# One attention and two expert layers on one core: the order of the whole program taken from a list scheduler written into the kernel, with buffers placed by hand

## The chip, the cores and the metric

One Trainium2 chip, one core of it. The metric is the device time in microseconds of one execution on that core. The kernel before takes 1005.12 us (median of 3 runs, 1003.41 to 1005.69).

## The reference

```python
# attention, batch 4, heads 8, sequence 576, head size 64
q_d, k_d, v_d = means over 4 neighbouring positions (144 of them)
out_up    = repeat(softmax(q_d k_d^T / 8) v_d, 4)
out_local = softmax(where(|i-j| < 4, q k^T / 8, -1e9)) v
x = (out_up + out_local)                     # 2304 tokens x 512
# first expert layer, 512 -> 1536 -> 512
xn = x / sqrt(mean(x*x) + 1e-6) * rms_g
g = xn @ w_gate
x = (g * sigmoid(g) * (xn @ w_val)) @ w_out
# second expert layer, 512 -> 2048 -> 512
r = maximum(x @ w_in, 0)
out = (s * (r * r) + b) @ w_out2
```

The first softmax is over scores with their row maximum subtracted, and its sum has 1e-9 added. The second layer's weights are called in_moe_w_in (or moe2_w_in) and in_moe_w_out among the kernel's inputs, like those of the first.

## The kernel before

The 2304 tokens are 8 blocks of 288. Activations lie transposed (features on partitions). Float32 products are made of fp16 halves: each operand is split into a high half (ACT, L133) and a low half (DVE, L134; or POOL, L136), and three fp16 products are accumulated. Weights arrive as 8-byte numbers: each 128-row piece is staged by a DMA (L476) and narrowed by two ACT and two DVE instructions (L480, L481, L485, L487); a product of the weights' upper halves with themselves ("gram", L515 for the first layer, L870 for the second) gives a bound from which the scale of the split is taken, so that no split can start before its part's gram.

- **Attention** runs per batch `b` and pair of heads (a "unit", 4 per batch): scores of the local windows (L357 and L361, tile sl), their maximum and its subtraction on DVE (L263, L264), exponent on ACT, sums and division; downsampled scores (L387, sd); transposes (L371, L407); products with the values (L278 for the downsampled ones, pvd, 12 matmuls on values that POOL has summed over 4 rows; L292 for the local ones, pl); then per half batch a norm (L425 to L451), whose factor is spread over the partitions by nine bf16 matmuls (L441). During batch 0 dummy matmuls (L319, `warm`) are issued in fixed numbers.
- **First expert layer, "moe1"** (L577 and L600): per block 24 groups of 12 matmuls 128x288 for gate and value (12 pairs), tanh on ACT and two products on DVE (L585, L187; tile u), halves of the result by ACT (L588) and POOL (L589), then 4 groups of 36 matmuls for the output. Blocks 0 and 1 run together part by part (4 weight parts), then blocks 2 to 5 singly, then 6 and 7 together. At a block's end a sum of squares (tile sn, L620) gives the scale of its result.
- **Second expert layer, "stage 2"** (L1123): a seven-product Strassen scheme on 2x2 blocks, so that a block of tokens takes 56 products of 12 matmuls 128x144; the first 28 (tiles bmm, bc) make the hidden values of four parts p, and the last 28 (by, bc) the outputs. Between them DVE and ACT form sums (L1141, L1145), squares, and halves (L1152, L1150). The eight weight parts, q0 to q3 of w_in and q4 to q7 of w_out2, each give 14 pieces 128x256, which are split after the part's gram. The halves of the hidden values need a scale (gsc, L895) that takes the grams of all eight parts.

**What sets the order.** The first 50 steps of the loop of blocks 0 and 1 (`run_first`, `ORDERED`) and all before them are ordered by the framework's own scheduler. After that PE's order is the program's, where generators of the main chain, of attention and of weight preparation are interleaved by hand-set numbers (`LAG_*`, `UNIT_STEP`, `START2`, ...; L35 to L60). Stage 2 is ordered by a small list scheduler `Plan` (PE, ACT and DVE; L1030 to L1085) with prices written into each call.

## Time and profile before

| what | value |
|---|---|
| median of the runs | 1005.12 us (1003.41 to 1005.69, n=3) |
| profiled execution, its own time | 1004.8 us |
| its span on the core | 1002.9 us |
| mean granted TensorE clock | 0.968 of full speed |
| busy: PE / DVE / ACT / POOL | 939.8 / 706.1 / 611.0 / 249.2 us |
| first moe1 matmul, first stage-2 matmul | 91.5, 653.5 us after the span's start |

The span runs from the first to the last instruction; the profiled execution's own time is 1.9 us longer. Busy time is the time in which an engine executes anything; overlapping instructions are counted once. The granted clock is TensorE's, as a share of 2.4 GHz.

### The profile page before, as it was taken

To read this page: it belongs to the slowest core of one execution; us is meant where nothing else is said; L and a number is where in the kernel's file an instruction comes from. 1 tells how busy PE (TensorE), PEld (TensorE's weight loads), DVE (VectorE), ACT (ScalarE), POOL (GpSimd) and SP (SyncE) were. 2 spreads that over 40 slices of the span, in tenths; PEclk is the share of its full clock that TensorE was granted. 3 is DMA by queue.
4 is the path that set the end of the run, shared out by engine and by line. 5 is a ranking of instruction groups with operands and counts; after the bars stand their busy time and mean duration, and the time that the engine had idled before them with its cause. 6 is when DMAs were issued, how large, how long until landed. Compare 5 with 4: busy or idle time off the path is not lost.

```text
span 1002.9 us, 27332 instructions
## 1 busy us (share of the span) xinstructions
PE 939.8 (94%) x11467; PEld 809.9 (81%) x11467; DVE 706.1 (70%) x1643; ACT 611.0 (61%) x1517; POOL 249.2 (25%) x341
## 2 busy tenths in 40 slices
PE   5975888979999999999999999689999999999998
PEld 3654766758877887878877888489999999999998
DVE  4997997764345244278686778879678796787966
ACT  2766687543444334356555555686769687686875
POOL 8524675544446333420211221000000000000000
PEclk9975999989999999999999999799999999999999
DMA  8982336211111100023220322000000000000000
GB/s 245 286 244 57 106 109 187 63 50 57 55 49 38 50 15 2 1 85 95 75 85 2 102 68 86 22 2 9 20 26 2 25 8 20 26 2 25 8 20 26
DMA packets 25580, 61.45 MB, mean 61 GB/s; under 512 B 3216, under 2 KB 11408, under 8 KB 25456
## 3 DMA queue, kind: packets, MB, share of 16 engines
q1 hardware_dynamic: 25456, 59.70, 19.6%
q8 instruction: 90, 1.47, 0.6%
q14 instruction: 34, 0.28, 0.1%
HBM read 54.97 MB, written 4.72 MB: 60 GB/s over the span
## 4 chain that ended last, share of the span: by engine, by line
PE 69%; DVE 16%; ACT 6%; DMA 3%; issue 3%; POOL 2%; SPq 0%; ACTq 0%; DVEq 0%; POOLq 0%
PE bc L1123 14%; PE mmb L577 13%; PE bmm L1123 12%; PE mmb L600 8%; PE by L1123 7%; DVE W L134 4%; PE m2b L577 4%; ACT W L133 2%; DVE u L585 1%; DVE u L187 1%; PE pl L292 1%; PE tpl L371 1%; PE m2b L600 1%; PE sl L361 1%; DVE W L487 1%
## 5 line engine op out<-in xcount | busy, mean ns | idle before, releaser
L1123 PEld LDWEIGHTS <-W 128*128 128x128 f16 x4704 | 297.2, 98 | 3.6 <-issue 3.6
L577 PEld LDWEIGHTS <-W 128*128 128x128 f16 x2304 | 223.3, 98 | 62.1 <-issue 5.4
L577 PE MATMUL mmb<-X,W 128*128 128x288 f16 x1752 | 236.3, 288 | 3.7 <-DVE u L585 1.9
L600 PEld LDWEIGHTS <-W 128*128 128x128 f16 x1152 | 113.1, 100 | 44.2 <-issue 8.0
L1123 PE MATMUL bmm<-W,W 128*128 128x144 f16 x1920 | 131.8, 226 | 1.6 <-DVE R L1141 1.6
L589 POOL TENSOR_TENSOR R<-u,R 128x288 f16<-128x288 f32 x96 | 78.1, 814 | 202.0 <-ACT R L588 186.1
L600 PE MATMUL mmb<-R,W 128*128 128x288 f16 x864 | 114.9, 289 | 6.6 <-DVE z L266 5.8
L588 ACT ACTIVATE R<-u 128x288 f16<-128x288 f32 x96 | 42.3, 441 | 87.1 <-DVE u L187 86.9
L1123 PE MATMUL bc<-W 128*128 128x144 f16 x1152 | 77.2, 226 | 0.0
L577 PE MATMUL m2b<-X,W 128*128 128x288 f16 x552 | 75.1, 286 | 0.0
L1152 DVE SCALAR_TENSOR_TENSOR W<-R,gsc,W 128x288 f16<-128x288 f32 x136 | 68.1, 511 | 4.5 <-ACT W L1150 4.5
L1150 ACT ACTIVATE W<-R,gsc 128x288 f16<-128x288 f32 x136 | 68.8, 523 | 3.1 <-DVE R L1141 2.1
L134 DVE SCALAR_TENSOR_TENSOR W<-W,wis 128x256 f16<-128x256 f32 x98 | 46.5, 505 | 23.2 <-ACT W L133 23.2
L1145 ACT ACTIVATE R<-R 128x288 f32<-128x288 f32 x160 | 62.7, 431 | 0.1
L585 DVE SCALAR_TENSOR_TENSOR u<-u,mmb 128x288 f32<-128x288 f32 x50 | 22.5, 450 | 55.7 <-PE mmb L577 52.8
L1123 PE MATMUL bc<-W,W 128*128 128x144 f16 x768 | 58.5, 226 | 1.7 <-ACT x L606 1.7
L1123 PE MATMUL by<-W 128*128 128x144 f16 x864 | 59.2, 228 | 0.0
L133 ACT ACTIVATE W<-W,wis 128x256 f16<-128x256 f32 x98 | 45.6, 500 | 19.0 <-DVE W L134 10.5
L1141 DVE TENSOR_TENSOR R<-bmm,R 128x288 f32<-128x288 f32 x72 | 32.6, 454 | 33.8 <-PE bmm L1123 21.9
L584 ACT ACTIVATE u<-mmb,tsc 128x288 f32<-128x288 f32 x96 | 47.1, 490 | 13.5 <-PE mmb L577 13.2
L487 DVE SCALAR_TENSOR_TENSOR W<-W,R 128x512 int32<-128x512 int32 (+1 forms) x53 | 46.4, 876 | 2.4 <-ACT W L480 1.3
L485 DVE SCALAR_TENSOR_TENSOR R<-R 128x512 int32<-128x512 int32 (+1 forms) x57 | 41.7, 733 | 7.7 <-ACT R L481 7.5
(260 smaller groups left out, 1606.8 us busy)
## 6 DMA issues: line engine op xcount, KB each, us to landing
R<-in_moe_w_out_dram SPq DMA_DIRECT2D x26, 512.0 KB
R<-in_moe_w_in_dram SPq DMA_DIRECT2D x16, 512.0 KB
qkT<-in_qk_dram SPq DMA_DIRECT2D x14, 576.0 KB
vw<-in_vwin_dram SPq DMA_DIRECT2D x14, 315.0 KB
vd<-in_vgrp_dram SPq DMA_DIRECT2D x13, 288.0 KB
W<-in_moe_w_gate_dram SPq DMA_DIRECT2D x9, 384.0 KB
R<-in_moe_w_val_dram SPq DMA_DIRECT2D x8, 384.0 KB
W<-in_moe_w_val_dram SPq DMA_DIRECT2D x8, 384.0 KB
```

Source lines behind the costliest of these rows:

```text
L133: act.activation(out=hi, in_=src, func=AF.Copy, scale=scale)
L134: dve.scalar_tensor_tensor(out=lo, in0=src, scalar=scale, in1=hi, op0=ALU.mult, op1=ALU.subtract)
L487: dve.scalar_tensor_tensor(out=di, in0=di, scalar=3, in1=stg[:, :, 0], op0=ALU.logical_shift_left, op1=ALU.bitwise_or)
L577: pe.matmul(out=acc, lhsT=Cgv.half(o, FP, lw)[:, f0 * 128:f0 * 128 + 128], rhs=X16[:, kc, 3 * blk:3 * blk + 3, lx, :], start=i == 0, stop= ...
L584: act.activation(out=u, in_=ps[0], func=AF.Tanh, scale=tsc[:, part:part + 1])
L588: act.activation(out=hi, in_=u, func=AF.Copy)
L589: pool.tensor_tensor(out=lo, in0=u, in1=hi, op=ALU.subtract)
L600: pe.matmul(out=acc, lhsT=Co.half(fc * 512, 512, lw)[:, m * 128:(m + 1) * 128], rhs=g16(fc)[:, lx, :], start=i == 0, stop=i == 35)
L1123: pe.matmul(out=p[:, m, :], lhsT=t[:, a:a + 128], rhs=x[:, i, lx, k, :], start=first and m == k == lw == lx == 0, stop=last_ and k == 1 an ...
L1145: plan.add(ACTe, lambda: act.activation(out=slot(o), in_=get(a), func=func), [nm(a)], [o], 0.34 if psum else 0.42, 0.45 if psum else 0.52)
L1150: plan.add(ACTe, lambda: act.activation(out=dst[:, i, 0], in_=s(), func=AF.Copy, scale=scale), [sn], [f"{dn}{i}h"], 0.43, 0.6)
L1152: plan.add(DVEe, lambda: dve.scalar_tensor_tensor(out=dst[:, i, 1], in0=s(), scalar=scale, in1=dst[:, i, 0], op0=ALU.mult, op1=ALU.subtrac ...
```

## The change

Every operation of the kernel (five engines: PE, ACT, DVE, POOL and SP's DMA issues) is no longer issued but recorded, with the spans of memory that it reads and writes (a PSUM bank counts as one). `schedule` gives each a duration by a formula, runs a list scheduler backward for due times and forward for the order, twice, and `emit` issues everything in that order, engine by engine. The main chain of matmuls (moe1 and stage 2) keeps the program's own order; everything else may go around it. Operations marked `either` go to DVE or POOL as the scheduler finds. DVE operations with two SBUF inputs and POOL operations are never scheduled at the same time. Dependences are those of the recorded order of the program: an operation that writes a buffer comes after all earlier ones that read it there.

All buffers are fixed: PSUM banks are MM (4), SB_ (2) and XV (2), handed out in turn by `take`; for blocks 5 to 7 moe1 also uses SB_ and the first XV bank. The grams and the sums sn use XV. `AREA` holds the attention's buffers first and the w_in parts later.

Three pieces of arithmetic move. For batches 0 and 1 (`PE_SUM`) the subtraction of the maximum is a float32 matmul with a negative identity (128x350 and 128x280), and the sum of 4 value rows is taken by 48 instead of 12 pvd matmuls per unit. The norm's factor is spread by three float32 matmuls instead of nine bf16 ones. The dummy matmuls become fillers that `emit` puts into gaps of the planned PE order before the first chain matmul.

DVE has 1755 instructions instead of 1643, POOL 143 instead of 337; PE's, ACT's and SP's numbers change little. All recorded operations are issued from line L292, fillers from L1033.

```diff
-ORDERED = 50
...
+PE_SUM = (0, 1)
...
+    def record(self, engs, name, args, kw):
+        if self.AP is None:
+            self.AP = type(args[0] if args else kw["out"])
...
+        for e in engs:
+            if e == "DVE":
+                occ = 0.065 + 1.042e-3 * n + (0.06 if scal else 0)
+                alts.append((e, occ, occ + 0.15, len(big) > 1 and n > 32))
+            elif e == "ACT":
+                psum = any(a.space == PSUM for a in ins)
+                occ = 0.06 + (0.85e-3 if psum else 0.95e-3) * n + 0.1 * scal + (0.09 if "accum_out" in kw else 0)
+                alts.append((e, occ, occ + 0.17, False))
+            elif e == "POOL":
+                occ = (0.9 if kw.get("op") == ALU.pow else 0.2) if n < 32 else 0.08 + 2.1e-3 * n * (0.9 if n > 500 else 1)
+                alts.append((e, occ, occ + 0.15, n >= 32))
...
+    def pe_time(self, name, kw):
+        n = cols(kw["out"])
+        rhs = kw.get("rhs", kw.get("in_"))
+        k = rhs.ap[0][1]
+        if name == "transpose":
+            return 0.11
+        if rhs.dtype == F32:
+            return 4 * n / 2.4e3 + 0.004 if k > 72 and n > 8 else 0.112 if k > 72 else n / 2.4e3 + 0.01
+        return n / 2.4e3 + 0.0024
...
+        while len(order) < n:
+            best = None
+            for e in engs:
+                w = wait[e]
+                w[:] = [x for x in w if not done[x[1]]]
+                ok = [x for x in w if e != "PE" or not self.ops[x[1]].chain or x[1] == chain[at]]
+                if not ok:
+                    continue
+                t = max(free[e], min(x[0] for x in ok))
+                lok = [x for x in ok if x[0] <= t + 1e-9]
+                k, i = min(((x[1], x[2]) for x in lok), key=lambda x: (key[x[0]], x[0]))
+                a = self.ops[k].alts[i]
+                ts = max(t, port) if a[3] else t
+                if a[3] and port > t + 0.05:
+                    other = [(x[1], x[2]) for x in lok if not self.ops[x[1]].alts[x[2]][3]]
+                    if other:
+                        k, i = min(other, key=lambda x: (key[x[0]], x[0]))
+                        ts = t
+                if best is None or ts < best[0] - 1e-9:
+                    best = (ts, e, k, i)
+            t, e, k, i = best
+            a = self.ops[k].alts[i]
+            done[k] = True
+            free[e] = t + a[1]
+            if a[3]:
+                port = t + a[1]
+            start[k], where[k] = t, i
+            if self.ops[k].chain:
+                at += 1
+            order.append(k)
+            for j in succ[k]:
+                if back:
...
+        for _ in range(rounds):
+            s, _w, _o, _t = self.run(succ, pred, chain[::-1], key, True)
+            late = [-(s[k] + self.ops[k].alts[0][1]) for k in range(n)]
+            start, where, order, t = self.run(pred, succ, chain, late, False)
+            if best is None or t < best[3]:
+                best = (start, where, order, t)
+            key = [-x for x in start]
...
+        for k in order:
+            o = self.ops[k]
+            e = o.alts[where[k]][0]
+            if e == "PE":
+                gap = start[k] - free
+                if free > until and start[k] <= first and gap > 0.5:
+                    for _ in range(int(0.7 * gap / 0.22)):
+                        filler()
+                free = start[k] + o.alts[0][1]
+            for name, args, kw in o.fn:
+                getattr(self.real[e], name)(*args, **kw)
...
+    MM, SB_, XV = bank[0:4], bank[4:6], bank[6:8]
...
-    def sum4(vd, vs=None):
-        pool.tensor_tensor(out=vd[:, :, 0:2, :], in0=vd[:, :, 0:2, :], in1=vd[:, :, 2:4, :], op=ALU.add)
-        if vs is None:
-            vs = ap.tile([72, 4, D], F32, tag="vs", name="vs", bufs=2)
-        pool.tensor_tensor(out=vs, in0=vd[:, :, 0, :], in1=vd[:, :, 1, :], op=ALU.add)
-        return vs
...
-        dve.tensor_tensor(out=a, in0=src, in1=zb, op=ALU.subtract)
...
+        if b in PE_SUM:
+            pe.matmul(out=src, lhsT=neg_f, rhs=zb, start=False, stop=True, skip_group_check=True)
+            act.activation(out=a, in_=src, func=AF.Exp, scale=1.0 / 8)
+        else:
+            dve.tensor_tensor(out=a, in0=src, in1=zb, op=SUB)
...
-    def warm(b, t, n):
-        if b < WARMB:
-            for _ in range(n):
-                pe.matmul(out=t, lhsT=ones_b, rhs=warm_in[:, :t.shape[1]], start=True, stop=True, skip_group_check=True)
...
+        if b not in PE_SUM:
+            pool.tensor_tensor(out=v4[:, :, 0:2, :], in0=v4[:, :, 0:2, :], in1=v4[:, :, 2:4, :], op=ADD)
+            vs = take("vs", VS)[:72].rearrange("p (a d) -> p a d", a=4)
+            pool.tensor_tensor(out=vs, in0=v4[:, :, 0, :], in1=v4[:, :, 1, :], op=ADD)
+            parts = [[vs[:, a, :]] for a in range(4)]
+        else:
+            parts = [[v4[:, a, r, :] for r in range(4)] for a in range(4)]
+        pvd = (take("mm0", MM[:3]) if b == 0 else take("xv", XV))[:, :SD]
...
+                        pe.matmul(out=pvd[64 * h:64 * h + 64, c0:c0 + n], lhsT=v,
...
-                pe.matmul(out=rb[:, c * GR:(c + 1) * GR], lhsT=rp[i][:, c:c + 1].to_broadcast([GR, 128]),
-                          rhs=ident_b[:GR, :GR], start=i == 0, stop=i == 2)
...
+                pe.matmul(out=rb[:, c * GR:(c + 1) * GR], lhsT=r[:, c:c + 1].to_broadcast([GR, 128]),
+                          rhs=ident_f[:GR, :GR], start=True, stop=True)
...
+    def mm_bank(t):
+        if wide_mm[0]:
+            return take("mmw", MM + SB_ + [XV[0]])
+        return take("mm", MM)
...
+            act.activation(out=g[:, fc, 0, :], in_=u, func=AF.Copy)
+            either.tensor_tensor(out=g[:, fc, 1, :], in0=u, in1=g[:, fc, 0, :], op=SUB)
...
+    HOME = [(AREA, q * PART) for q in range(4)] + [(W1, q * PART) for q in range(3)] + [(R, 0)]
...
-        first = mains((0, 1))
-        sides.append(attn(1))
-        run_first(first, 0, ORDERED)
-        order[0] = tc.manual_schedule(engines={pe.engine})
-        order[0].__enter__()
-        run_first(first, ORDERED, 1000)
...
+    for hp in range(NP):
+        unit(0, hp)
+    for hh in range(2):
+        norm(0, hh)
+    def attention(b):
+        for hp in range(NP):
+            unit(b, hp)
+        for hh in range(2):
+            norm(b, hh)
+    prep_gv(0)
+    g = [g16_of(0), g16_of(1)]
+    for part in range(NPART):
+        if part:
+            prep_gv(part)
+        for blk in range(2):
+            moe1_gv(blk, g[blk], part)
+    prep_out()
+    attention(1)
+    for blk in range(2):
+        moe1_out(blk, g[blk])
+    for blk in range(2, NB - 2):
+        if blk in (2, 3):
+            attention(blk)
+        if blk == NB - 3:
+            wide_mm[0] = True
+            for q in range(4):
+                prep_part(q)
+        g = g16_of(blk)
+        for part in range(NPART):
+            moe1_gv(blk, g, part)
+        moe1_out(blk, g)
+    g = [g16_of(0), g16_of(1)]
+    for part in range(NPART):
+        for i in range(2):
+            moe1_gv(NB - 2 + i, g[i], part)
+    for i in range(2):
+        moe1_out(NB - 2 + i, g[i])
+    x_ops(0)
+    for q in range(4, 8):
+        prep_part(q)
+    part_scales()
     for blk in range(NB):
         in_stage(blk)
         if blk == 0:
-            last_post()
-            finish_out2()
+            bias()
         if blk < NB - 1:
             x_ops(blk + 1)
         y_stage(blk)
-    plan.emit()
-    order[0].__exit__(None, None, None)
-    tail["pw"].__exit__(None, None, None)
...
+    with tc.manual_schedule(engines={nc.tensor.engine, nc.scalar.engine, nc.vector.engine, nc.gpsimd.engine, nc.sync.engine}):
+        plan.emit(filler, 4.0)
```


In the order of instructions, three places. The first is DVE around the first use of moe1's gate and value results, before and after. Names: W is the weights' space, R and u are working buffers (R also holds staging), rs the scales of the gate and value splits, gvh, gvs, gvi the steps of a scale, tsc the factor of the tanh. A 128x384 operation with rs is a low half of a gate or value piece; one without is a narrowing.

Before, from the first low half on (the first u operation, L585, is row 161, with the narrowings of part 1 and the norm of the second half batch between):

```order
134 L134 SCALAR_TENSOR_TENSOR W_82<-W_82,rs 128x384
135 L183 TENSOR_SCALAR gvi<-gvs 128x2
136 L521 TENSOR_SCALAR rs<-rms_sb,gvs 128x4 x2
137 L296 TENSOR_TENSOR X<-pl,od 128x256
138 L134 SCALAR_TENSOR_TENSOR W_82<-W_82,rs 128x384
139 L522 TENSOR_SCALAR tsc<-gvi 128x1
140 L187 SCALAR_TENSOR_TENSOR invg<-gvi 128x1
141 L134 SCALAR_TENSOR_TENSOR W_82<-W_82,rs 128x384 x6
142 L296 TENSOR_TENSOR X<-pl,od 128x320
143 L134 SCALAR_TENSOR_TENSOR W_82<-W_82,rs 128x384 x7
144 L296 TENSOR_TENSOR X<-pl,od 128x256
145 L134 SCALAR_TENSOR_TENSOR W_82<-W_82,rs 128x384
```

After, the start of the splits, and the piece up to the first u operations (rows 183 and 187):

```order
139 L292 TENSOR_SCALAR rs<-rms_sb,gvs_162 128x4
140 L292 TENSOR_REDUCE m_152<-bank_101 128x1
141 L292 SCALAR_TENSOR_TENSOR W_85<-W_85,R 128x384
142 L292 TENSOR_SCALAR rs<-rms_sb,gvs_162 128x4
143 L292 TENSOR_SCALAR gvi_163<-gvs_162 128x2
144 L292 TENSOR_REDUCE m_152<-bank_100 128x1
145 L292 SCALAR_TENSOR_TENSOR W_85<-W_85,rs 128x384 x4
146 L292 TENSOR_SCALAR m_152<-m_152,rmax 128x2
147 L292 SCALAR_TENSOR_TENSOR W_85<-W_85,rs 128x384
```

```order
176 L292 SCALAR_TENSOR_TENSOR W_85<-W_85,rs 128x384 x7
177 L292 TENSOR_REDUCE AREA<-bank_100 128x3
178 L292 TENSOR_SCALAR rs<-rms_sb,gvs_165 128x4
179 L292 SCALAR_TENSOR_TENSOR W_85<-W_85,rs 128x384
180 L292 TENSOR_SCALAR AREA<-AREA 128x3
181 L292 SCALAR_TENSOR_TENSOR W_85<-W_85,rs 128x384 x2
182 L292 SCALAR_TENSOR_TENSOR R<-R 128x512
183 L292 SCALAR_TENSOR_TENSOR u_89<-u_89,bank_95 128x288
184 L292 SCALAR_TENSOR_TENSOR W_85<-W_85,R 128x512
185 L292 SCALAR_TENSOR_TENSOR W_85<-W_85,rs 128x384
186 L292 TENSOR_SCALAR AREA<-AREA 128x3
187 L292 SCALAR_TENSOR_TENSOR u_89<-u_89,bank_94 128x288
```

The narrowings of all four parts (64 operations 128x384 on DVE) and 26 of the 32 low halves now stand ahead of the first complete u; before, 59 narrowings and 16 low halves on DVE did.

The second place is DVE at the start of stage 2. Before (L134 are the last 14 of the 112 low halves 128x256, L1141 is stage 2's first sum, gsc the scale of the hidden values):

```order
861 L187 SCALAR_TENSOR_TENSOR mm__8409<-invj,ivw 128x4
862 L892 TENSOR_REDUCE big<-mm__8409 128x1
863 L893 TENSOR_SCALAR big<-big 128x1
864 L895 TENSOR_SCALAR gsc<-mm__8409,big 128x4
865 L134 SCALAR_TENSOR_TENSOR R<-R,wis 128x256 x14
866 L187 SCALAR_TENSOR_TENSOR c_8469<-s_sb,big 128x1
867 L187 SCALAR_TENSOR_TENSOR cy<-cx,c_8469 128x7
868 L1141 TENSOR_TENSOR R<-bmm,R 128x288 x3
869 L1141 TENSOR_TENSOR R<-bc,R 128x288
870 L1141 TENSOR_TENSOR R<-bmm,R 128x288
871 L1141 TENSOR_TENSOR R<-bc,R 128x288 x2
872 L1152 SCALAR_TENSOR_TENSOR W_82<-R,gsc,W_82 128x288
```

After, the start of stage 2 (mo is the maximum of block 7's sn, mi that of a gram in bank 100 or 101, the row with bank_95 is stage 2's first sum) and then the place of gsc:

```order
945 L292 TENSOR_REDUCE mo<-bank_101 128x1
946 L292 TENSOR_SCALAR poh_180<-mo 128x1
947 L292 TENSOR_SCALAR pos_181<-poh_180 128x1
948 L292 TENSOR_REDUCE mi<-bank_100 128x1
949 L292 TENSOR_TENSOR W_85<-W_85 128x2x256
950 L292 TENSOR_SCALAR wih_183<-mi 128x1
951 L292 TENSOR_TENSOR W_85<-W_85 128x2x256
952 L292 TENSOR_SCALAR wis_184<-wih_183 128x1
953 L292 TENSOR_REDUCE mi<-bank_101 128x1
954 L292 TENSOR_TENSOR R<-bank_95,R 128x288
955 L292 SCALAR_TENSOR_TENSOR W_85<-W_85,wis_184 128x256 x2
956 L292 TENSOR_SCALAR wii_185<-wis_184 128x1
```

```order
1008 L292 TENSOR_REDUCE big<-mm_157 128x1
1009 L292 SCALAR_TENSOR_TENSOR R<-R,wis_187 128x256
1010 L292 TENSOR_SCALAR big<-big 128x1
1011 L292 SCALAR_TENSOR_TENSOR W_85<-W_85,wis_184 128x256
1012 L292 TENSOR_SCALAR gsc<-mm_157,big 128x4
1013 L292 SCALAR_TENSOR_TENSOR W_85<-W_85,wis_184 128x256
1014 L292 SCALAR_TENSOR_TENSOR R<-R,wis_187 128x256 x2
1015 L292 SCALAR_TENSOR_TENSOR W_85<-R,gsc,W_85 128x288 x5
1016 L292 SCALAR_TENSOR_TENSOR W_85<-W_85,wis_184 128x256 x2
1017 L292 SCALAR_TENSOR_TENSOR R<-R,wis_187 128x256
```

Before, 98 of the 112 low halves stand ahead of gsc and of stage 2's first sum; now 56 stand ahead of the first sum, and the other 56 (rows 955 to 1062) between it and the first output product, with gsc at row 1012 among them. Between row 954 and row 1070, where the last halves stand that the first output product takes, there are these 56 low halves, 29 low halves of stage-2 operands, 38 sums 128x288, and 24 others, 147 in all.

## Rows read from the trace of the kernel before

**Rows 1.** The page: busy time of each engine.

```profile
PE 939.8 (94%) x11467; PEld 809.9 (81%) x11467; DVE 706.1 (70%) x1643; ACT 611.0 (61%) x1517; POOL 249.2 (25%) x341
```

**Rows 2.** Windows, five stages: stretch, length, busy (instructions) by engine, PEclk, DMA share, GB/s.

```profile
0.00:91.50 91.50, 62.15 (x709) 43.44 (x710) 71.80 (x162) 51.60 (x131) 47.70 (x70) 0.80 0.73 219
91.50:217.20 125.70, 109.45 (x1161) 84.44 (x1160) 105.86 (x227) 87.67 (x219) 73.79 (x82) 0.96 0.36 109
217.20:600.00 382.80, 380.69 (x3727) 305.40 (x3728) 214.84 (x490) 183.47 (x449) 124.30 (x186) 0.99 0.17 51
600.00:664.00 64.00, 52.85 (x475) 42.29 (x473) 51.10 (x120) 39.73 (x94) 3.38 (x4) 0.92 0.14 42
664.00:998.60 334.60, 334.60 (x5401) 334.34 (x5398) 262.06 (x645) 247.59 (x628) 0.00 (x0) 0.99 0.05 15
```

**Rows 3.** Timeline, PE, moe1's first matmuls and the wait of block 0's output: start, us, what.

```profile
91.53 1.84 PE L577 MATMUL mmb<-X,W 128*128 128x288 f16 x7 [1.09 <-ACT X L450]
...
210.24 1.14 PE L577 MATMUL mmb<-X,W 128*128 128x288 f16 x8
217.20 0.66 PE L600 MATMUL mmb<-R,W 128*128 128x288 f16 x2 [5.82 <-DVE z L266]
```

**Rows 4.** Windows, the start, columns as in rows 2.

```profile
0.00:75.00 75.00, 56.06 (x654) 39.19 (x655) 59.61 (x139) 43.23 (x113) 40.18 (x58) 0.86 0.86 258
75.00:91.50 16.50, 6.08 (x55) 4.25 (x55) 12.18 (x25) 8.37 (x19) 7.52 (x12) 0.50 0.12 41
```

**Rows 5.** Timeline, DVE: neighbours in a dense stretch.

```profile
60.10 0.55 DVE L485 SCALAR_TENSOR_TENSOR R<-R 128x384 int32<-128x384 int32 x1
60.57 0.43 DVE L263 TENSOR_REDUCE z<-sl 128x4 f32<-128x280 f32 x1
...
61.01 0.52 DVE L485 SCALAR_TENSOR_TENSOR W<-W 128x384 int32<-128x384 int32 x1
61.45 0.54 DVE L487 SCALAR_TENSOR_TENSOR W<-W,R 128x384 int32<-128x384 int32 x1
```

**Rows 6.** Windows, line L577 alone: PE and PEld busy (instructions).

```profile
91.50:217.20 125.70, 79.11 (x576) 55.78 (x575) 0.96 0.36 109
```

**Rows 7.** Chain that ended last, two of its pieces: start, us, what.

```profile
457.19 4.41 PE mmb L600 x36
461.60 4.42 PE m2b L600 x36
```

**Rows 8.** Timeline, PE: value sums and downsampled scores of one unit.

```profile
326.58 0.88 PE L278 MATMUL pvd<-PdT,vs 72*64 72x64 f32 x24
327.39 1.89 PE L600 MATMUL mmb<-R,W 128*128 128x288 f16 x14
...
312.29 0.95 PE L387 MATMUL sd<-qd 64*64 64x144 f32 x12
313.17 1.03 PE L577 MATMUL mmb<-X,W 128*128 128x288 f16 x7
```

**Rows 9.** PE's waits: operation, line, releaser: total us, times, longest.

```profile
PE sn L620 <- ACT x L606: 7.6, 2, 6.1
...
PE mmb L600 <- DVE z L266: 5.8, 1, 5.8
```

**Rows 10.** Windows, start of stage 2, columns as in rows 2.

```profile
653.50:682.00 28.50, 25.18 (x473) 24.83 (x471) 23.20 (x63) 24.64 (x65) 0.00 (x0) 1.00 0.01 2
682.00:695.00 13.00, 13.00 (x185) 13.00 (x183) 11.68 (x34) 8.79 (x22) 0.00 (x0) 0.87 0.01 3
```

**Rows 11.** Windows, line L134 (DVE) alone, first of these stretches.

```profile
653.50:682.00 28.50, 5.80 (x14) 1.00 0.01 2
```

**Rows 12.** Timeline, PE: slow matmuls, stage 2's first product, its first output product.

```profile
636.27 7.28 PE L600 MATMUL m2b<-R,W 128*128 128x288 f16 x36
...
653.50 1.66 PE L1123 MATMUL bmm<-W,W 128*128 128x144 f16 x24
...
681.83 3.66 PE L1123 MATMUL by<-W 128*128 128x144 f16 x36
```

More of the change, by code (lines that the diff above doesn't have):

```diff
@@ L1112, in product, with pair_bank, put, tt @@
-    def product(ps, i, w, x, xn, first, last_):
+    YS = [two(AREA[:, NPART * PART + 512:]), SL[13], SL[11]]
+    KEEP = [two(X2[:, TB * i:TB * i + TB]) for i in range(2)]
+    BIN, BC, BY = MM, SB_, XV
+    def pair_bank(name, items):
+        return two(take(name, items)[:, :TB])
+    def put(dst, i, src, scale):
+        halves(dst[:, i, 0], dst[:, i, 1], src, scale)
+    def tt(o, a, b, op):
+        dve.tensor_tensor(out=o, in0=a, in1=b, op=op)
+    def product(ps, i, w, x, first, last):
@@ L1334 @@
[L1334 to L1343 removed]
+        tt(v, c, v, ADD)
```

1544 lines of the change are left out of this document (577 added, 967 removed).

## The prediction

> **What bounds the kernel now.** I read the busy line of the page first [rows 1]: TensorE (PE) is busy 939.8 of 1002.9 us, so at most about 60 us can be won without less matmul work. The windows by stage [rows 2] say where they lie. From 217.2 to 600 PE is busy 380.7 of 382.8 us, and from 664 to 998.6 all the time: in these 717 us an order can win 2 us. What is left is the start (PE busy 62.2 of 91.5 us, partly with dummy matmuls), the stretch in which blocks 0 and 1 run beside the attention of batch 1 (109.5 of 125.7 us), and the passage into stage 2 (52.9 of 64 us). The change can win in these three places, and lose anywhere.
>
> In the first two PE is not the one that works: DVE is busy 71.8 + 105.9 = 177.7 of 217.2 us, POOL 47.7 + 73.8 = 121.5 us beside it [rows 2]. The timeline shows their end [rows 3]: the first moe1 matmul starts at 91.53, the gate and value products of blocks 0 and 1 end at 211.4, and the first output matmul waits 5.82 us until 217.20, for DVE [rows 9]. In the passage PE waits 7.6 us for the sums of squares behind ACT [rows 9], and 36 matmuls take 7.28 us [rows 12] where they take 4.41 elsewhere [rows 7], at a clock below full speed; that is 2.8 us more. Stage 2 starts at 653.50 and its first output product at 681.83 [rows 12], 28.3 us later.
>
> I write the time as four stretches and two remainders, in span time: 217.2 to the first output matmul; 653.5 - 217.2 = 436.3 to stage 2; 28.3 to its first output product; 998.6 - 681.8 = 316.8 to PE's end; 1002.9 - 998.6 = 4.3 for the last results, and 1.9 between the span and the execution's own 1004.8 us. The median of the runs, 1005.12, is 0.3 us above that, which I neglect.
>
> **The start, to the first output matmul.** The order puts nearly all narrowing of all four gate and value parts ahead of the first moe1 matmul. The transfers for it ran at 258 GB/s until 75 us, then at 41 [rows 4]; so what was loaded by 75 us before is loaded no earlier now, and the last pieces' narrowing, their gram and the first splits follow. I take the first moe1 matmul at 80 us, between 76 (nothing but a few operations behind the transfers) and 92 (as before).
>
> From there PE has to do what it did in 91.5 to 217.2, and more. The 109.45 us busy [rows 2] count the 576 gate and value matmuls as 79.11 us [rows 6], but back to back such a matmul takes 4.41 / 36 = 0.1225 us [rows 7], 70.6 us in all; the difference of 8.5 us is overlap or waiting, and 101 us of work remain. Batch 1 gets dearer: 48 pvd matmuls instead of 12. The 12 take 327.39 - 326.58 = 0.81 us [rows 8], so each unit gains 2.4 us. No row has a float32 matmul of 128 partitions and hundreds of columns, as the subtraction of the maximum now is. The nearest is the downsampled scores, six of 144 columns in 0.88 us [rows 8], 1.02 ns per column; for 350 + 280 columns that is 0.64 us, the lower end, and twice that, 1.3, the upper (twice the rows are used). I take 0.7. Four units: 4 x 3.1 = 12.4 us. PE therefore needs 80 + 101 + 12.4 = 193.4 us; with 1.6 us for waits **195 us**, a gain of 22.
>
> The condition is that DVE keeps up. It has to issue 422 instructions to the last u of block 1, before 386. At the old price, 177.7 us for the 389 that started by 217.2 [rows 2], 0.457 us each, that makes 193 us, plus some 6.5 us until the first weights are there: DVE would have to be busy without a gap and would end at 199. In a dense stretch DVE's operations start closer than they last: two narrowings 0.44 us apart, each 0.52 to 0.55 long [rows 5]. Costing all 422 by such distances gives about 150 us. So DVE ends between 157 and 199, plus its waits, and PE's 195 stands only if there are few of them. POOL's lost work (194 instructions fewer in the whole kernel) is not waited for elsewhere. Low end for this stretch 183, high end 214.
>
> By the Trainium skill ("SBUF — State Buffer", section "SBUF: two separate sides") a DVE operation with two SBUF inputs and a GpSimd operation that reads SBUF hold a shared port pair exclusively, so that the other waits; taking work from POOL would by that rule give DVE time back, and the sum of this stretch would lie nearer its low end. The trace does not show a lock over all work: DVE and POOL together were busy 179.7 us in 125.7 [rows 2].
>
> **From there to stage 2.** PE's work is nearly the same: the norm's fewer matmuls and the moved weight preparation make about 1 us less. Attention of batches 2 and 3 is again spread among the blocks. Before, PE had 2.1 us of waits to 600 [rows 2]; a fixed order by formula durations I give about the same 2 us. The 7.6 us for sn [rows 9] should go, since ACT no longer makes splits beside blocks 6 and 7, and the slow clock of 2.8 us behind that wait with it. A fixed order that misjudges some durations may cost 1 to 6 us; I take 2. 436.3 - 1 - 7.6 - 2.8 + 2 = **427 us**, a gain of 9; ends 424 to 433.
>
> **The start of stage 2.** Here the change loses. The grams of q4 to q7 use the XV banks, which moe1's accumulators and sums hold to the end of block 7, so that they and all 56 pairs of splits stand behind stage 2's first sum. Before, 14 were left [rows 11]. The scale gsc, without which no hidden value can be halved, now comes after more than half of these splits. DVE's rows 954 to 1070, which the first output product must await, are 147 instructions. The 14 splits took 5.80 us, 0.414 each [rows 11]; the other 49 instructions of that stretch 23.20 - 5.80 = 17.4 us [rows 10], 0.355 each. So DVE needs 56 x 0.414 + 91 x 0.355 = 23.2 + 32.3 = 55.5 us. PE has 28.3 us of work there, products, grams and bias, and waits out the rest. ACT was busy 24.64 of 28.5 us [rows 10] and gets the same 42 high halves more. By starting distances in place of durations DVE would need 51 us, the low end; coupled waits of ACT and DVE put the high end at 62. I take **55 us**, a loss of 26.7. From then on PE's products are the same: 316.8 us, 4.3 and 1.9 stay. The clock fell to 0.87 behind the short waits before [rows 10], and will again; I cost it at no difference.
>
> **The sum.** 195 + 427 + 55 + 316.8 + 4.3 + 1.9 = **1000.0 us**, 4.8 below the profiled execution, 0.5% below the median. Two large terms nearly cancel: 22 + 9 won, 27 lost.
>
> **The rivals.**
> 1. *Slower: DVE sets the start.* If its operations keep the price of 0.457 us, DVE ends at 199 at best, and at 212 if it is idle 13 us, a third of the 39.5 us (217.2 - 177.7) that it was idle before. Deciding point: the first output matmul later than about 200 us. For it speaks that DVE gets the low halves and sums that POOL made, and that PE sees the first complete u only behind 26 splits; against it that POOL disturbs less. The time is 1000 + 17 = 1017 us; with the high end of stage 2's start as well 1024.
> 2. *Faster: DVE is relieved by POOL's quiet.* If exclusion by POOL is what made DVE's operations longer than their distances, the two DVE-bound terms fall: the start to 185, where PE limits with a first matmul at 76 and a cheaper subtraction, and stage 2's start to 50. The time is 1000 - 10 - 5 = 985 us. The rule of the skill cited above would make it so. Stage 2 had no POOL work at all [rows 2], which speaks against the second half.
> 3. *The wait at stage 2 is hidden:* if DVE gets far into the splits while PE is still in block 7, because banks come free earlier than the order suggests. The order of each engine is fixed, so at most a few rows can move; 40 us instead of 55 would give 985 us as well.
> 4. *The orders drift apart:* PE stands in a planned order, and float32 matmuls on 64 to 72 rows are priced by formula at about half of what the trace shows. Waits of attention would then stand in the middle of the chain, 10 us in place of 2: 1008 us.
>
> **How the numbers follow.** A measurement of this kernel can tell about 0.2%, 2 us, from no change. My forecast, between 990 and 1003, gets 0.38; rival 1 (1010 to 1026) 0.28; rivals 2 and 3 together (975 to 990) 0.18; rival 4 and small mixtures (1003 to 1010) 0.16. Faster by over 0.2% (below 1003.1) is the forecast, and rivals 2 and 3, less the edge: 0.54. Within 0.2% (1003.1 to 1007.1): 0.11. Slower: 0.35. The range for 8 in 10 takes the low ends of start and stage 2 together on one side, 183 + 424 + 51 + 323 = 981, with 5 us for ends that are too high, 976; and on the other rival 1 with its high end and a little drift, 1026. The forecast's own range is 990 to 1003.
>
> **What would show it.** Right: first moe1 matmul near 80 us with DVE dense from about 7 us on, first output matmul near 195 with no 5.8 us wait, no wait of sn at the end of block 7, and then a gap of some 27 us in all on PE before the first bias product or the first output product of stage 2, its releaser DVE or ACT at the splits 128x256; from there 100% PE. Wrong: a first output matmul later than 205 (rival 1), gaps of PE between 217 and 650 of over 5 us (rival 4), or a first output product less than 45 us behind stage 2's start (rivals 2 and 3).

## The result, and the profile after

The changed kernel takes 1013.33 us (median of 4 runs, 1011.92 to 1013.99) against 1005.16 for the kernel before beside it: a ratio of 1.0082, 95% interval 1.0065 to 1.0100. It is 0.8% slower. I had put 0.35 on that side and forecast 1000.0; the measured time lies inside the range, 976 to 1026.

The busy line of the page after, for [rows 1]:

```profile
PE 971.5 (96%) x12044; PEld 844.9 (83%) x12044; DVE 706.5 (70%) x1755; ACT 606.6 (60%) x1518; POOL 120.0 (12%) x147
```

TensorE (PE) is busy 31.7 us longer than before, with the same matmuls in the main chain. POOL is down from 249.2 to 120.0 us, and DVE, which took over some of its work, has not grown: 706.5 us. The windows of the stages, cut at the same events as [rows 2] (columns: stretch, length, busy of PE, PEld, DVE, ACT, POOL with instructions, PEclk, DMA share, GB/s):

```profile
0.00:107.60 107.60, 85.52 (x1073) 62.68 (x1074) 75.47 (x187) 61.22 (x154) 29.94 (x49) 0.97 0.69 206
107.60:235.20 127.60, 121.63 (x1412) 99.55 (x1410) 97.49 (x234) 82.63 (x200) 34.03 (x37) 0.97 0.31 93
235.20:600.00 364.80, 364.53 (x3575) 293.79 (x3574) 217.32 (x539) 174.75 (x430) 54.81 (x60) 1.00 0.18 53
600.00:651.30 51.30, 51.30 (x422) 40.97 (x420) 27.19 (x58) 20.15 (x45) 1.20 (x1) 1.00 0.17 53
651.30:691.30 40.00, 31.98 (x535) 31.54 (x533) 36.63 (x108) 33.50 (x87) 0.00 (x0) 0.87 0.01 2
691.30:1007.90 316.60, 316.56 (x5040) 316.38 (x5040) 251.90 (x631) 233.46 (x604) 0.00 (x0) 1.00 0.06 16
```

The timeline of PE after gives the events (start, us, operation; idle time before it and its releaser in brackets): the first matmul, a value sum of batch 0 and what follows it, the first moe1 matmul, the longest wait in moe1, the first output matmul.

```profile
16.31 0.80 PE L292 MATMUL bank<-u,ones_f 128*128 128x128 f32 x2 [16.31 <-DVE u L292]
```
```profile
76.88 4.85 PE L292 MATMUL bank<-AREA 72*64 72x64 f32 x96
81.66 0.60 PE L1033 MATMUL bank<-mask,ones_b 128*128 128x512 bf16 x2
```
```profile
107.59 3.10 PE L292 MATMUL bank<-X,W 128*128 128x288 f16 x24
...
119.94 0.37 PE L292 MATMUL bank<-AREA 70*64 70x64 f32 x2 [5.32 <-ACT AREA L292]
```
```profile
235.24 1.02 PE L292 MATMUL bank<-R,W 128*128 128x288 f16 x7
```

And around the start of stage 2: the first product, two waits for DVE, the first output product, for [rows 12].

```profile
651.29 0.91 PE L292 MATMUL bank<-W,AREA 128*128 128x144 f16 x12
...
669.83 7.04 PE L292 MATMUL bank<-W,AREA 128*128 128x144 f16 x84 [2.13 <-DVE wii L292]
...
686.28 3.04 PE L292 MATMUL bank<-W,AREA 128*128 128x144 f16 x24 [5.61 <-DVE X L292]
...
691.29 1.02 PE L292 MATMUL bank<-W 128*128 128x144 f16 x7 [0.28 <-DVE bt L292]
```

My four stretches and remainders, in us:

| stretch | before | forecast | after |
|---|---|---|---|
| start to first output matmul | 217.2 | 195 | 235.2 |
| of it, to the first moe1 matmul | 91.5 | 80 | 107.6 |
| from there to stage 2 | 436.3 | 427 | 416.1 |
| stage 2 to its first output product | 28.3 | 55 | 40.0 |
| to PE's end | 316.8 | 316.8 | 316.6 |
| to the span's end, and outside it | 6.2 | 6.2 | 6.1 |

So the start lost 18 us where I had it win 22, the middle won 20, and stage 2's start lost 12. In the middle PE is busy 364.5 + 51.3 of 416.1 us; the waits of [rows 9] are gone. In 107.6 to 235.2 PE is idle 6 us, all of them in the first 22 us, where DVE has no gap; from 130 us on PE has none:

```profile
107.60:130.00 22.40, 16.43 (x153) 12.47 (x151) 22.40 (x58) 19.99 (x47) 4.97 (x5) 0.85 0.17 52
130.00:235.20 105.20, 105.20 (x1261) 87.08 (x1260) 75.09 (x177) 62.64 (x154) 29.06 (x32) 1.00 0.33 102
```

So most of this stretch is PE's work, and one row names a large part of what is new in it. The 48 pvd matmuls of a unit take 81.66 - 76.88 = 4.78 us after, where 12 took 0.81 [rows 8]; over the 8 units of batches 0 and 1 that is 4.0 x 8 = 32 us. PE's busy time grew by as much, but that is in part chance: the subtractions of the maximum came on top (the operations with neg_f, 6.8 + 5.5 = 12.3 us over 8 units), so other work on PE got shorter. Three groups by form up to 260 us, the fillers first (busy us, mean ns | idle before):

```profile
L1033 PE MATMUL bank<-mask,ones_b 128*128 128x512 bf16 x89 | 25.2, 414 | 0.0
L292 PE MATMUL bank<-AREA,neg_f 128*128 128x350 f32 x16 | 6.8, 508 | 0.1
L292 PE MATMUL bank<-AREA,neg_f 128*128 128x280 f32 x16 | 5.5, 425 | 0.0
```

### The profile page after: what moved, and what is told of

Read it like the earlier page. It is cut to its first block, busy times and chain, and to the rows that moved or that the text cites. A ratio compares the mean times of both kernels' runs of the same rounds, so it can differ in the third digit from the quotient of the medians.

```text
span 1012.2 us, 28289 instructions
## 1 busy us (share of the span) xinstructions
PE 971.5 (96%) x12044; PEld 844.9 (83%) x12044; DVE 706.5 (70%) x1755; ACT 606.6 (60%) x1518; POOL 120.0 (12%) x147
## 4 chain that ended last, share of the span: by engine, by line
PE 88%; DVE 8%; ACT 2%; DMA 1%; issue 1%; ACTq 0%; DVEq 0%; SPq 0%
PE bank L292 87%; DVE W L292 3%; DVE R L292 2%; DVE AREA L292 1%; DMA R<-in_moe_w_in_dram 1%; PE bank L1033 1%; ACT W L292 1%; ACT R L292 1%; DVE X L292 1%; DVE m L292 0%; DVE u L292 0%; ACT AREA L292 0%; DMA R<-in_moe_w_val_dram 0%; DVE mi L292 0%; DVE rs L292 0%
## 5 line engine op out<-in xcount | busy, mean ns | idle before, releaser
L292 PEld LDWEIGHTS <-W 128*128 128x128 f16 (+1 forms) x5712 | 478.1, 98 | 91.6 <-issue 5.6
L292 PE MATMUL bank<-X,W 128*128 128x288 f16 (+2 forms) x2400 | 300.7, 284 | 0.7 <-DVE u L292 0.7
L292 PEld LDWEIGHTS <-AREA 128*128 128x128 f16 (+1 forms) x2752 | 175.6, 99 | 8.6 <-issue 8.3
L292 PE MATMUL bank<-W,AREA 128*128 128x144 f16 x2688 | 173.5, 228 | 7.7 <-DVE X L292 5.6
L292 PE MATMUL bank<-W 128*128 128x144 f16 (+1 forms) x2160 | 146.9, 227 | 2.5 <-DVE m L292 1.9
L292 PE MATMUL bank<-R,W 128*128 128x288 f16 (+2 forms) x1248 | 147.8, 281 | 0.0
L292 DVE SCALAR_TENSOR_TENSOR u<-u,bank 128x288 f32<-128x288 f32 x192 | 86.0, 448 | 35.0 <-PE bank L292 32.5
L292 ACT ACTIVATE R<-R 128x288 f32<-128x288 f32 (+3 forms) x226 | 103.7, 492 | 3.6 <-DMA R<-in_moe_w_out_dram 2.6
L292 POOL TENSOR_TENSOR AREA<-AREA 128x576 f32<-128x576 f32 (+5 forms) x73 | 68.9, 950 | 227.9 <-PE bank L292 107.4
L292 PE MATMUL bank<-AREA 70*64 70x64 f32 (+5 forms) x1888 | 87.6, 229 | 5.6 <-ACT AREA L292 5.3
L292 DVE TENSOR_TENSOR R<-bank,R 128x288 f32<-128x288 f32 x128 | 57.6, 452 | 48.9 <-PE bank L292 35.4
L292 PEld LDWEIGHTS bank<-AREA 72*64 72x64 f32 (+2 forms) x1824 | 75.9, 138 | 15.6 <-ACT AREA L292 7.1
L292 ACT ACTIVATE AREA<-bank 72x384 f32<-72x384 f32 (+5 forms) x98 | 42.0, 447 | 73.9 <-PE bank L292 71.1
L292 ACT ACTIVATE X<-bank 128x288 f32<-128x288 f32 (+2 forms) x93 | 34.6, 408 | 82.0 <-PE bank L292 82.0
L292 ACT ACTIVATE R<-u 128x288 f16<-128x288 f32 x96 | 41.9, 438 | 62.3 <-DVE u L292 62.2
L292 ACT ACTIVATE W<-R,gsc 128x288 f16<-128x288 f32 x136 | 68.6, 524 | 0.6 <-DVE R L292 0.5
L292 DVE SCALAR_TENSOR_TENSOR W<-R,gsc,W 128x288 f16<-128x288 f32 x136 | 68.0, 508 | 1.1 <-ACT W L292 1.1
L292 DVE TENSOR_REDUCE mo<-bank 128x1 f32<-128x288 f32 x8 | 3.6, 455 | 87.0 <-PE bank L292 87.0
L292 ACT ACTIVATE u<-bank,tsc 128x288 f32<-128x288 f32 x96 | 47.6, 496 | 22.7 <-PE bank L292 21.7
L292 DVE SCALAR_TENSOR_TENSOR R<-R 128x512 int32<-128x512 int32 (+1 forms) x66 | 45.6, 698 | 18.4 <-ACT R L292 18.1
L292 PE MATMUL bank<-R 128*128 128x144 f16 (+3 forms) x760 | 55.2, 226 | 0.0
L292 DVE TENSOR_TENSOR R<-u,R 128x288 f16<-128x288 f32 x74 | 34.6, 468 | 21.1 <-ACT R L292 20.6
```

The source lines that it names most:

```text
L292: getattr(self.real[e], name)(*args, **kw)
```

## The experiments

Ratios are to runs of the kernel before on the same chip, with 95% intervals. Each experiment was ordered anew by the kernel's own scheduler, so more than the edited lines can move. Differences between experiments are differences of medians; on the chips that they ran on the kernel before took 1003.7 to 1005.2 us, so such a difference is uncertain by 1 to 2 us. Event times are those of the one profiled execution of each.

**1. Value sums back on POOL.**

```diff
-        if b not in PE_SUM:
+        if True:
             pool.tensor_tensor(out=v4[:, :, 0:2, :], in0=v4[:, :, 0:2, :], in1=v4[:, :, 2:4, :], op=ADD)
```

> The sum of 4 value rows goes back to POOL for batches 0 and 1 (12 instead of 48 pvd matmuls per unit), all else as in the changed kernel, the scheduler reorders by itself. Theory A, PE work on the path: a unit's pvd takes 0.8 us instead of 4.85, 4.0 us x 8 units = 32 us less PE work, nearly all of it on the path, because PE is what the chain of waits passes through from 21 us on: 981 to 987 us, first moe1 matmul at 92 to 97 us instead of 107.6. Theory B, the start is set by the late loads and by narrowing all four weight parts first: the first moe1 matmul stays at 104 or later and only batch 1's 16 us are won: about 997 us. Theory C, POOL's return disturbs DVE by as much: 1008 or more.

991.25 us, ratio 0.9883 (0.9868 to 0.9899): 22 us below the changed kernel, and faster than the kernel before. The first moe1 matmul comes at 97.9 us, the first output matmul at 214.2, 21 us earlier; everything behind it moves along. That is most of what theory A expected, short of its 26 to 32. The new order also puts PE's first matmul at 6.0 us instead of 16.3; experiment 4 shows that such an earlier start alone wins nothing in the changed kernel. The windows to the first output matmul:

```profile
0.00:97.90 97.90, 73.78 (x799) 48.05 (x800) 82.84 (x190) 59.47 (x151) 41.72 (x57) 0.98 0.76 231
97.90:125.00 27.10, 19.24 (x158) 13.82 (x156) 26.13 (x60) 22.39 (x51) 5.86 (x5) 0.87 0.20 62
125.00:214.20 89.20, 88.67 (x981) 70.48 (x979) 74.04 (x175) 61.20 (x153) 32.52 (x36) 1.00 0.35 109
```

In the 27.1 us after the first moe1 matmul DVE is busy 26.1 and PE 19.2: there DVE sets the pace. From 125 us on PE is busy 88.7 of 89.2 us.

**2. The maximum's subtraction back on DVE as well.**

```diff
-        if b in PE_SUM:
+        if False:
             pe.matmul(out=src, lhsT=neg_f, rhs=zb, start=False, stop=True, skip_group_check=True)
```

> Both pieces of arithmetic go back (PE_SUM empty in effect: the maximum is subtracted on DVE, the value rows are summed on POOL). Theory A: beside the 32 us of pvd, 8 times some 1.3 us of float32 matmuls leave PE, against 16 DVE subtractions of 0.45 to 0.5 us: 976 to 984 us, 3 to 6 us below the run with the sum alone on POOL. Theory B: within 3 us of that run or above it, since DVE has 7.5 us more work in the stretch that it sets.

995.79 us, ratio 0.9921 (0.9904 to 0.9939): 4.5 us above experiment 1, the side of theory B. The first output matmul is at 218.4, 4.2 us later. PE lost work there and DVE gained 16 subtractions, so this half of the moved arithmetic is a gain: it costs PE time and gives DVE back some.

**3. The grams of w_out2 earlier.**

```diff
-            return take("mmw", MM + SB_ + [XV[0]])
+            return take("mmw", MM + SB_)
...
-    for i in range(2):
-        moe1_out(NB - 2 + i, g[i])
-    x_ops(0)
-    for q in range(4, 8):
-        prep_part(q)
+    for q in range(4, 7):
+        prep_part(q)
+    moe1_out(NB - 2, g[0])
+    prep_part(7)
+    moe1_out(NB - 1, g[1])
+    x_ops(0)
```

> Only the start of stage 2 is changed: moe1's blocks 5 to 7 no longer take the first XV bank, and the preparation of q4 to q7 is recorded before the output matmuls of blocks 6 and 7, so that grams and splits can be scheduled beside them. If the late grams are what costs there, the time from stage 2's first product to its first output product falls from 40.0 to 28 to 31 us and the total by 9 to 12 us: 1001 to 1005. If the two fewer-bank rotation or DVE beside block 7 costs as much, PE waits move ahead of stage 2 and the total stays within 3 us of 1013.

1001.45 us, ratio 0.9970 (0.9957 to 0.9982): 12 us below the changed kernel. The windows before stage 2, of its start, and of the first block of output products and what follows:

```profile
600.00:658.70 58.70, 58.70 (x586) 47.26 (x584) 50.02 (x129) 37.81 (x89) 1.46 (x2) 0.97 0.16 46
658.70:680.20 21.50, 21.50 (x348) 21.40 (x345) 17.66 (x51) 15.74 (x44) 0.00 (x0) 1.00 0.01 2
680.20:722.20 42.00, 42.00 (x676) 42.00 (x673) 32.55 (x81) 30.74 (x81) 0.00 (x0) 1.00 0.06 16
```

Stage 2 starts 7.4 us later, since grams and bias products now stand ahead of it, but its first output product comes after 21.5 us without a wait, at 680.2 instead of 691.3. DVE's work moved to where DVE was idle: 50.0 us busy in 600 to 658.7, against 27.2 in 51.3 us. The edit takes a bank out of the rotation and records the grams earlier, both at once; which of the two had held the grams back it does not tell.

**4. Batch 0's attention first.**

```diff
+            late = [x - 1e4 * (k < self.early) for k, x in enumerate(late)]
             start, where, order, t = self.run(pred, succ, chain, late, False)
```

(`early` is the number of operations recorded before the first weight part.)

> Only priorities are changed: everything recorded before the first weight part (batch 0's attention, its loads, the scale of rms_g) goes first on every engine. Theory B: PE's first matmul comes at 4 to 6 us instead of 16.3, and the first moe1 matmul up to 11 us earlier: 1003 to 1009 us. Theory A: PE starts earlier, but the weights are then narrowed later by as much; the first moe1 matmul at 103 to 112 us, 1009 to 1018 in all.

1014.56 us, ratio 1.0117 (1.0094 to 1.0140). The first matmul is at 7.8 us instead of 16.3, the first moe1 matmul at 100.8 instead of 107.6, but the first output matmul at 234.0, hardly moved. The late start is real, but bringing it forward wins nothing.

**5, 6. The value sums on TensorE for one batch alone.**

```diff
-        if b not in PE_SUM:
+        if b != 0:
```

This is experiment 5, with the sums on PE for batch 0; experiment 6 has `b != 1`.

> The sum of 4 value rows on TensorE for batch 0 alone, on POOL for the others; tells where the 22 us of the run with the sum on POOL come from. If all of TensorE's extra work is paid wherever it stands: 4 units x 4.0 us = 16 us above that run, 1005 to 1009. If batch 0's stands in a start that DVE sets (narrowing of all four weight parts), only 0 to 6 us are paid: 991 to 997, and the other 16 belong to batch 1.

> The counterpart: the sum on TensorE for batch 1 alone, on POOL for the others. If PE's work is what ends last between the first moe1 matmul and the first output matmul, all of 4 x 4.0 us is paid: 1005 to 1009. If DVE ends last there, less: 992 to 1000. Together with the run for batch 0 the two surpluses should make about 22 us.

1001.1 us, ratio 0.9981 (0.9964 to 0.9998), and 1005.7 us, ratio 1.0016 (1.0005 to 1.0028): 10 and 14 us above experiment 1, together 24. The first output matmul comes at 227.1 and 225.6 instead of 214.2. Batch 1's share is paid nearly in full (14 of 16 us), and batch 0's costs more than the 0 to 6 us that I expected if DVE set the start. Four units cost 10 to 14 us wherever they stand. Which batch pays more is not shown: the medians say batch 1, the first output matmuls of the two profiled executions batch 0 (experiment 5's profiled execution took 1005.57 us, 4.5 above its median).

**7. Without the fillers.**

```diff
-                        filler()
+                        pass
```

> The changed kernel without its 89 fillers (25.2 us of PE busy time before the first chain matmul); they compute nothing. If they stand in the way of real matmuls: 2 to 8 us faster than 1013. If they only hold the clock: the granted clock in the first 110 us falls below 0.97 and the kernel is 1 to 8 us slower. Theory A (PE's real work) expects within 4 us of 1013.

1016.36 us, ratio 1.0122 (1.0106 to 1.0137), 3 us slower than the changed kernel. The granted clock of the first 109 us:

```profile
0.00:109.00 109.00, 75.70 (x982) 65.36 (x983) 76.80 (x190) 61.97 (x156) 29.54 (x49) 0.79 0.66 203
```

It is 0.79 instead of 0.97. So the fillers hold the clock, and taking them away wins nothing. The clock is worth only 3 us here: without the fillers the first moe1 matmul moves from 107.6 to 109.1 and the first output matmul from 235.2 to 237.8.

**8. Experiments 1 and 3 together.**

> Both repairs together: value sums on POOL and the grams of q4 to q7 beside blocks 6 and 7. If the two costs lie in different stretches they add: 991.3 - 12 = 979 us, between 977 and 982. If the second gives way to the first (DVE beside block 7 filled by what was late before): 984 to 991.

978.86 us, ratio 0.9749 (0.9733 to 0.9765): the two repairs add up, 991.25 - 12, as far as the uncertainty of 1 to 2 us tells. The windows of its stages:

```profile
0.00:99.20 99.20, 73.86 (x790) 48.59 (x800) 82.18 (x190) 59.20 (x151) 41.81 (x57) 0.98 0.74 227
99.20:214.20 115.00, 107.51 (x1136) 84.30 (x1134) 99.50 (x234) 83.43 (x203) 37.84 (x41) 0.97 0.33 100
214.20:637.20 423.00, 422.69 (x4185) 341.60 (x4184) 271.31 (x685) 217.97 (x532) 59.37 (x66) 1.00 0.17 52
637.20:658.70 21.50, 21.50 (x347) 21.40 (x345) 17.68 (x51) 15.74 (x44) 0.00 (x0) 1.00 0.01 2
658.70:973.90 315.20, 315.16 (x5043) 314.97 (x5040) 242.71 (x597) 227.46 (x589) 0.00 (x0) 1.00 0.06 16
```

From 214.2 us on PE is busy 759.4 of 759.7 us. All that is left to an order lies ahead of that.

**9 to 11. On top of both repairs:** attention first (as in 4), prices of small float32 matmuls by the trace, and no rule that keeps POOL and DVE apart.

```diff
-            return 4 * n / 2.4e3 + 0.004 if k > 72 and n > 8 else 0.112 if k > 72 else n / 2.4e3 + 0.01
+            return 4 * n / 2.4e3 + 0.004 if k > 72 and n > 8 else 0.112 if k > 72 else max(0.068, n / 1e3)
```

```diff
-                alts.append((e, occ, occ + 0.15, len(big) > 1 and n > 32))
+                alts.append((e, occ, occ + 0.15, False))
...
-                alts.append((e, occ, occ + 0.15, n >= 32))
+                alts.append((e, occ, occ + 0.15, False))
```

> On top of both repairs, batch 0's attention, its loads and the scale of rms_g go first on every engine. In the changed kernel itself this brought the first moe1 matmul 7 us earlier and nothing to the time, because PE and DVE filled the gain after it. With 32 us of PE work gone the start is less full: if the late first loads now count (PE's first scores at 13.5 us, 7.8 in the kernel before), 972 to 976 us; if DVE's narrowing ends last in any order, 977 to 983.

> On top of both repairs, the formula prices float32 matmuls on up to 72 rows by the trace (at least 0.068 us, 1 ns per column) instead of about half. My rival 4 said that wrong prices make PE's fixed order wait: then 2 to 6 us faster, 973 to 977. If the order has enough slack between DVE and PE: within 2 us of 979.

> On top of both repairs, the scheduler no longer keeps POOL operations and DVE operations with two SBUF inputs apart; it will give POOL more and let both run at once. If they exclude each other on the chip, DVE's operations get longer beside POOL and the plan is missed: 981 to 990 us. If they hardly disturb each other, the relieved DVE shortens the start: 970 to 977 us.

Attention first: 977.46 us, ratio 0.9723 (0.9701 to 0.9745). Prices: 979.19, ratio 0.9741 (0.9720 to 0.9761). Neither can be told from experiment 8. So wrong prices of small matmuls are not what costs. My rival 4 falls with that, and with PE's waits in the changed kernel: between 235 and 651 us they come to 0.3 us.

Without the rule: 990.27 us, ratio 0.9858 (0.9841 to 0.9876), 11 us slower than experiment 8, with POOL busy 180.3 instead of 139.0 us. The first output matmul comes at 221.5 instead of 214.2. DVE's narrowings up to 214 us, grouped by form (busy us, mean ns), in experiment 8:

```profile
L292 DVE SCALAR_TENSOR_TENSOR W<-W 128x384 int32<-128x384 int32 x28 | 18.6, 690 | 0.1
...
L292 DVE SCALAR_TENSOR_TENSOR W<-W,R 128x384 int32<-128x384 int32 x18 | 11.5, 649 | 0.2
L292 DVE SCALAR_TENSOR_TENSOR R<-R 128x384 int32<-128x384 int32 x18 | 10.5, 599 | 5.2 <-ACT R L292 5.1
```

and in this one:

```profile
L292 DVE SCALAR_TENSOR_TENSOR W<-W 128x384 int32<-128x384 int32 x28 | 17.3, 633 | 0.6 <-ACT W L292 0.3
L292 DVE SCALAR_TENSOR_TENSOR R<-R 128x384 int32<-128x384 int32 x18 | 13.2, 741 | 5.1 <-ACT R L292 5.1
L292 DVE SCALAR_TENSOR_TENSOR W<-W,R 128x384 int32<-128x384 int32 x18 | 13.0, 728 | 0.2
```

Two forms grew by 12 and 24%, one shrank by 8%. These means mix two cases that the traces keep apart. Of the 64 narrowings in experiment 8, the 36 with no POOL operation beside them last 0.52 to 0.56 us; of the 26 with one beside them for over half their time 11 last longer than 0.65 us, up to 1.50. In experiment 11 it is 17 of 27, up to 1.63, and the 32 with none last 0.54 to 0.56. One of the long ones of experiment 8, with a short one ahead of it and POOL beside:

```profile
76.24 0.54 DVE L292 SCALAR_TENSOR_TENSOR R<-R 128x384 int32<-128x384 int32 x1
76.70 1.50 DVE L292 SCALAR_TENSOR_TENSOR W<-W,R 128x384 int32<-128x384 int32 x1
...
75.39 2.41 POOL L292 TENSOR_TENSOR AREA<-AREA,mhalf 96x3 f32<-96x3 f32 x2 [0.56 <-DVE AREA L292]
77.77 2.19 POOL L292 TENSOR_TENSOR AREA<-AREA 128x576 f32<-128x576 f32 x2
```

So POOL does hold up narrowings. That explains little of the 11 us: the narrowings' busy time grew from 40.6 to 43.5 us. By which way the scheduler's rule is worth the rest is not settled, since the order changed as well (PE's first matmul at 21.3 us instead of 6.0).

**12, 13. On top of both repairs, weight parts 1 to 3 put off.**

```diff
+            for (a, p), (b, _) in zip(self.marks[::2], self.marks[1::2]):
+                for k in range(a, b):
+                    late[k] += 20 * p
```

(`marks` are the first and last operations of `prep_gv(part)`; experiment 13 has 30 for 20.)

> On top of both repairs, the due times of weight parts 1, 2 and 3 (loading, narrowing, splits) are put off by 20, 40 and 60 us, so that DVE's first complete u stands behind 51 narrowings and 8 low halves instead of 64 and 24. If narrowing everything first is what holds the start (theory B), the first moe1 matmul comes at 80 to 90 us instead of 99.2, the early waits of PE for u go, and the total falls by 5 to 12 us: 967 to 974. If DVE's total work to the first output matmul ends last in any order, that matmul stays at 212 to 217 us and the total within 3 us of 979.

> The same with 30, 60 and 90 us: 35 narrowings and 8 low halves before the first complete u. If theory B holds and the order is what counts: first moe1 matmul at 70 to 85 us, total 962 to 974; if the put-off parts then come too late for the chain, waits of PE for the low halves appear between 100 and 180 us and the total is above that of the run with 20.

986.7 us, ratio 0.9813 (0.9778 to 0.9847), 8 us slower than experiment 8, and 982.18, ratio 0.9770 (0.9745 to 0.9795), which cannot be told from it. The first moe1 matmul comes at 84.1 and 78.0 us instead of 99.2, as theory B would have it, and the first output matmul at 214.2 and 212.3, as before. Experiment 12's windows to there:

```profile
0.00:84.10 84.10, 62.06 (x732) 42.19 (x740) 71.88 (x165) 53.79 (x139) 37.66 (x55) 1.00 0.75 226
84.10:150.00 65.90, 62.69 (x555) 49.18 (x555) 59.48 (x142) 45.97 (x106) 13.88 (x14) 0.97 0.33 100
150.00:214.20 64.20, 53.11 (x582) 41.47 (x580) 42.32 (x96) 39.99 (x100) 23.01 (x26) 0.80 0.39 116
```

What is won ahead of 84 us is lost behind 150, where PE is busy 53.1 of 64.2 us at a clock of 0.80. More is lost behind the first output matmul, which is thus not the whole measure of the start: from it to stage 2's first product experiment 12 takes 429.2 us, experiment 8 423.0. The first 26 of these us, in experiment 8 and then in experiment 12, show the lower clock and fewer matmuls done:

```profile
214.20:240.00 25.80, 25.80 (x217) 20.41 (x216) 5.42 (x18) 6.05 (x19) 0.00 (x0) 1.00 0.01 1
214.20:240.00 25.80, 25.80 (x181) 20.11 (x181) 9.89 (x28) 7.31 (x20) 4.09 (x4) 0.83 0.12 36
```

Theory B is not borne out: narrowing later brings the first moe1 matmul forward, and no time is won by it. After the first moe1 matmul PE waits in experiment 12 mostly for ACT's results of the attention (7.9 us), not for weights (2.7 us).

## Why the prediction was wrong

- **The start: 195 us forecast, 235.2 measured. This is the step that failed,** in two of its terms. First, "Batch 1 gets dearer: 48 pvd matmuls instead of 12 ... each unit gains 2.4 us". The row after gives 4.0 us: 96 records of the trace (two for each float32 matmul) take 4.78 us, 0.050 each, where 24 took 0.81, 0.034 each. And I counted the four units of batch 1 alone; the edit is made for batch 0 too, whose cost I had hidden behind a start set by transfers. Experiments 1, 5 and 6 show that both batches pay: 22 us in all. The subtraction of the maximum, for which I took 0.7 us a unit, fills 12.3 / 8 = 1.5 us. Second, "I take the first moe1 matmul at 80 us" rested on transfers and on narrowing; it came at 107.6. The chain of waits of the first 130 us after, by line, has hardly a transfer in it; to 88 us it runs mostly over PE's attention, then to 127 us over DVE:

```profile
by line: PE bank L292 40.9%; DVE W L292 16.7%; PE bank L1033 6.5%; DVE R L292 6.0%; issue 4.6%; ACT W L292 3.9%; DVE AREA L292 3.3%; DVE m L292 3.1%; ACT R L292 3.0%; DMA R<-in_moe_w_val_dram 2.6%; DVE X L292 2.3%; ACT AREA L292 2.1%; DVE u
```

  Experiments 12 and 13 bring that event to 84 and 78 us and win nothing by it: it was the wrong event to argue from. Of the 40 us that the start was too long, experiment 1 takes away 21; what holds the other 19 (214.2 against 195) is not shown.
- **Rival 1, the DVE-bound start, at 1017 us,** came near the total by luck: its start of 212 us was 23 us too short, and its middle and stage 2's start together 26 too long. DVE has no gap in the first 22 us behind the first moe1 matmul and may set those, but from 130 us on it is PE that has none. Its price was about right: without the value sums DVE is busy 183.0 us to the first output matmul (experiment 1), 183.0 / 425 = 0.43 us per instruction, near the 0.457 that I took from before and far from the starting distances.
- **The middle: 427 forecast, 416.1 measured.** The waits for sn and the slow clock went, as forecast. A further 3.7 us are the 64 gram matmuls that moved behind stage 2's start. The drift of 2 us did not come, and the 2 us of old waits that I had kept went too: PE's waits in 235 to 651 are 0.3 us. The remaining 3 us I have not broken down.
- **Stage 2's start: 55 forecast, 40.0 measured; right in kind, too dear by 15.** DVE is busy 36.6 of the 40.0 us, PE's waits are for DVE, and having the grams earlier takes 12 us away (experiment 3). The wrong size came from "DVE's rows 954 to 1070, which the first output product must await". When that product starts, DVE has come to about row 1028, 99 of my 147 instructions; the product does not need the halves up to row 1070. The price was about right: these 99 take 35.0 us (656.25 to 691.29), 0.354 each, where 55.5 / 147 is 0.378. The 5 us from stage 2's first product to row 954 were not in my sum.
- **The rule of the Trainium skill on the shared port pair** ("SBUF — State Buffer", section "SBUF: two separate sides") would have moved my sum to an earlier start. The start came later, and the part of the delay that is explained is PE's. The traces agree with the rule as far as they go: narrowings, which read two SBUF inputs, are long only beside POOL (experiments 8 and 11). What the scheduler's ban of overlap is worth as a whole, 11 us, they do not explain by it.
- **Faster or slower:** two terms that I had nearly cancelling were both off, by +40 and by -15, and the middle by -11. Together +14, the difference between forecast and profile.

**Still open:** what holds the start of the repaired kernel. From 125 us to the first output matmul PE is busy 88.7 of 89.2 us there, as in experiment 1, so the time is lost ahead of that. Neither an earlier start (9) nor another order of the weight parts (12, 13) moves the first output matmul by more than 2 us. With other prices (10) it came at 208.2 us in the profiled execution, but the median of its runs is not lower. What brought it forward clearly was less work on PE. Whether DVE's sum of work or batch 1's chain of waits through ACT and DVE is the limit was not tried by itself.

The version with both repairs, 978.9 us, is 2.5% faster than the kernel before. So the rest of the change, the list scheduler, the placed buffers and the other moved arithmetic taken together, is a gain of some 25 us, and two details cost more than that, some 34 us: the value sums on PE, and the late grams of the last weight parts.
